# A block-wise 32x32 turn of attention's results on DVE, and w1 read in rows of 1 KB with one transfer per feature block

## The chip, the cores and the metric

The kernel runs on one core of a Trainium2 chip. What is measured is the device time of one execution in microseconds. A core has a matrix engine (PE, whose weight loads are listed apart as PEld), three engines for element-wise work (DVE, ACT, POOL), an engine that here does nothing but issue transfers (SP), and sixteen DMA engines that carry out the transfers. Each engine has its own instruction order and its list is worked through in that order; semaphores tell one engine when a result of another is there.

## The reference

Chunked attention is followed by a mixture of experts in which each token goes through all eight experts, weighted by a Sinkhorn routing.

```python
# attention: B=4, H=8, S=768, D=64; chunks of 32, context 16 left and 8 right, 8 memory tokens
for c in range(S // 32):
    q_c = q[:, :, c_start:c_end]
    k_full = concatenate([mem_k, k[:, :, l_start:r_end]])
    v_full = concatenate([mem_v, v[:, :, l_start:r_end]])
    a = softmax(q_c @ k_full.T / sqrt(D))          # per chunk
    out[:, :, c_start:c_end] = a @ v_full
x = out.transpose(0, 2, 1, 3).reshape(3072, 512)   # tokens x features
# mixture of experts: 8 experts, w_gate 512x8, w1 8x512x1024, w2 8x1024x512
P = exp(x @ w_gate - max)
for _ in range(8):
    P /= P.sum(1); P /= P.sum(0); P *= 3072 / 8
for e in range(8):
    out += P[:, e:e+1] * (maximum(x @ w1[e], 0) @ w2[e])
```

All inputs and outputs are float32 in HBM. 254.82 MB are moved in all; what counts most in arithmetic are the two products of each expert.

## The kernel before

**Attention.** The 3072 tokens are 24 blocks of 128 queries. For block n, q_n and k_n are loaded (L848, L842 to L845), kx_n, the context before and behind the block with the memory tokens (L782 to L790), and v (L921, into whatever room the planner has: v_pair, x_room, or a buffer of w2 that isn't used yet). PE turns q, k and kx (tq L1006, tk L1010, tx L806), ACT copies the turned k into kC (L1020), PE forms the scores (sp), DVE and ACT the softmax (L1083, L1089, L1108), PE turns the probabilities (ta L1126) and multiplies by v (xp L1136). DVE divides by the sums (L1154 to L1156) into xq, and the instruction at L1176 turns xq from queries x features to features x queries, in squares of 32x32, into xg, which holds 256 tokens. At the same line the features are dealt to four blocks kt: before the change, feature f of a head group went by `(f k)`, so that the four blocks take every fourth element.

**Experts.** Two xg make a unit of 512 tokens; there are six units. `build` splits x into a high and a low float16 half (ACT L513, DVE L521). The weights w1 and w2 of each expert are loaded in four parts (fp = 0 to 3) of 512 KB (`load`, L549 and L551), scaled by their largest element (`most`, L558, and `scales`), and split the same way. The first expert on the first units is done by plain products: pp (x by w1, L2037) and yp (h by w2, L2118). The others go by a scheme of seven products of 2x2 blocks (px, py, pz, then yx, yy, yz, L1590), for which `cut` adds and subtracts parts of the weights on POOL. For experts 1 to 7 all of w1 and w2 is loaded twice: once early for the largest element (w1fm, w2fm) and once for use. The routing's logits are products of xg with the gate's 512x8 weights (lp, L1391), loaded once at L2176.

**What sets the order.** Nothing waits for its turn dynamically. While the program is built, a planner takes all operations with a duration (the second argument of `add`), a priority (a due time), their dependencies and buffers, and lays out each engine's list as if those durations held. The lists that come out are fixed. Where the planner sees PE idle in the first part it puts in warm-up matmuls (`fill`, L427), whose results nobody reads. SP issues nearly all transfers, in the planned order; a transfer whose buffer isn't free holds up those behind it. So a changed duration or a changed number of instructions can move other operations to other places in the lists.

Of the kernel before, what the change touches and what calls it, by code (L numbers as in the profile page):

```python
# [233 lines left out]
def tile_chunked_attn_sinkhorn_moe(  # L234
# [27 lines left out]
    nc = tc.nc  # L262
    P = 128
    B, H, S, D = q.shape
    NM = mem_k.shape[2]
    N, DM = out.shape
    E, _, F = w1.shape
# [10 lines left out]
    KT = DM // P  # L278
# [249 lines left out]
        return b  # L528


    w1v = w1.rearrange("e (p kt) (fh fp f) -> e fp p kt fh f", p=P, fh=2, fp=FP)
    w2v = w2.rearrange("e (fh fp p) d -> e fp p fh d", fh=2, fp=FP)
    wo = {}
    known = {}

    def load(e, fp, which, prio, ahead="", eng="SP", after=()):
        shape = [P, 2, KT, P] if which == 1 else [P, 2, DM]
        place = "stage", stage
        if (e, which) == (0, 2) and ahead == "" and fp < 2:

            place = ("ws", "ss")[fp], comb
        st = buf(*place, shape, F32, f"w{which}f{ahead}_{e}_{fp}")

        queue = nc.scalar if eng == "ACT" else nc.sync

        def go():
            if which == 1:
                for fh in range(2):
                    queue.dma_start(st.t[:, fh], w1v[e, fp, :, :, fh])  # L549
            else:  # L550
                queue.dma_start(st.t, w2v[e, fp])  # L551

        return st, add(eng, 2 if which == 1 else 1, go, after, prio, [st], dma=2.1)

    def most(e, fp, which, st, deps, prio):
        def go():
# [37 lines left out]
    def cut(e, fp, which, st, ld, prio):  # L594
# [10 lines left out]
            return lambda: ws.t[:, i]  # L605

        if which == 1:
            a11, a12 = lambda: st.t[:, 0, 0:2], lambda: st.t[:, 0, 2:4]
            a21, a22 = lambda: st.t[:, 1, 0:2], lambda: st.t[:, 1, 2:4]
            ops = [  # L610
                (0, a21, a22, ALU.add),
                (1, part(0), a11, ALU.subtract),
                (2, a11, a21, ALU.subtract),
                (3, a12, part(1), ALU.subtract),
            ]
            shape = [P, 2, 7, 2, P]
        else:
            b11, b12 = lambda: st.t[:, 1, 0:DH], lambda: st.t[:, 1, DH:DM]
            b21, b22 = lambda: st.t[:, 0, 0:DH], lambda: st.t[:, 0, DH:DM]
            ops = [  # L620
                (0, b12, b11, ALU.subtract),
                (1, part(0), b22, ALU.subtract),
                (2, b22, b12, ALU.subtract),
                (3, b21, part(1), ALU.add),
            ]
            shape = [P, 2, 7, DH]
# [8 lines left out]
        if which == 1:  # L635
            parts = [
                (
                    lambda j: o.t[:, j, 0:2].rearrange("p o k f -> p (o k) f"),
                    lambda: st.t[:, 0],
                    (0.72, 0.85),  # L640
                ),
                (lambda j: o.t[:, j, 2], a22, (0.5, 0.65)),
# [45 lines left out]
    def plain1(fp, st, ld, prio):  # L688

        o = operands("w1", [P, 2, 7, 2, P], f"w1_0_{fp}")  # L690
        done = split(
            lambda j: o.t[:, j, 0:4].rearrange("p o k f -> p (o k f)"),
            lambda: st.t.rearrange("p a k f -> p (a k f)"),
            sw[:, 0, 0:1],
            [known[0, 1], ld],
            prio,
            (1.15, 1.28),
            [st, o],
        )
        wo[0, fp, 1] = (o, [done])  # L700


    def block1(e, i):
# [408 lines left out]
    def values(n, s, made):  # L1112
# [62 lines left out]
        def turn_out():  # L1175
            nc.vector.transpose(  # L1176
                gt.t[:, :, o : o + QB].rearrange("p k (c q) -> p k c q", c=CB),
                xq.t.rearrange("p c a (f k) -> p k c (a f)", k=KT),
            )

        t = add("DVE", 0.72, turn_out, [t], at + 2, [xq, gt])
        halves[g][1].append(t)
        if n % (GT // QB) == GT // QB - 1 and g > 1:

# [986 lines left out]
    for fp, s in enumerate(fetch_first(1, START)):  # L2171
# [1 line left out]
    gate_in[0] = add(  # L2173
        "SP",
        1,
        lambda: nc.sync.dma_start(  # L2176
            gate[:, :, 0:E], w_gate.rearrange("(p kt) e -> p kt e", p=P)
        ),
        (),
        30.0,  # L2180
        dma=0.3,
# [138 lines left out]
```

## Time and profile before

| | |
|---|---|
| three runs | 1918.31, 1921.56, 1921.51 us; median 1921.51 |
| the profiled execution | 1922.6 us, of which 1920.8 us are the span of the profile |
| HBM read and written over the span | 187.84 MB and 63.44 MB, 131 GB/s |
| chain that ended last, by engine | PE 93%, DVE 4%, DMA 1%, issue 1%, SP's queue 1% |
| the seven-product matmuls (px, py, pz, yx, yy, yz, L1590) | 273 ns each |
| yp (L2118) | 576 matmuls of 379 ns, 132.2 us |
| w1f, issues on SP | 72 of 256 KB |
| w1fm, issues on SP | 56 of 256 KB |

The profile is one execution, recorded instruction by instruction. The share of busy time of an engine tells what it did and not what it cost: an engine that is off the chain can be busy all the time for nothing. Three kinds of views help here: tables that split the span into stages and give each engine's busy time in each stage with PE's granted clock; lists of instructions in order of time, in which a bracket gives the idle time ahead of an instruction and what ended it; and groups of like instructions with their count, their total and their mean. In such rows "x8" is a count, "128x512 f32" the partitions, the elements per partition and the type, and SPq stands for the issuing of transfers by SP.

### The profile page before, as it was taken

The numbers are of one execution on the slowest core, as the hardware profiler recorded it, in microseconds if no ns is written. First come the engines' busy times: TensorE is split into PE (matmuls) and PEld (weight loads), VectorE is DVE, ScalarE is ACT, GpSimd is POOL, SyncE is SP. The second block draws the span as 40 slices with busy tenths as digits, with TensorE's granted clock in tenths as the row PEclk, the third lists the DMA queues.
The fourth block names the chain that finished last, engine by engine and source line by source line (L and its number), as shares of the span: only waits on it lengthen the run. The fifth ranks groups of instructions, "written<-read, shape, count | busy, mean of one in ns | idle before, by whom it ended". The sixth has DMA issues, their size and how long they took to land.

```text
span 1920.8 us, 47137 instructions
## 1 busy us (share of the span) xinstructions
PE 1899.4 (99%) x19546; PEld 1634.9 (85%) x19546; DVE 1464.2 (76%) x2420; ACT 1021.5 (53%) x1995; POOL 524.2 (27%) x549
## 2 busy tenths in 40 slices
PE   8999999999999999999999999999999999999999
PEld 7676676688888888888888888888888888888888
DVE  6886778878769866898778875898678885786565
ACT  4664554656556545645545554654554564564453
POOL 1220012543224231442124231342124232332112
PEclk9999999999999999999999999999999999999999
DMA  8677663453235332255214533245413632322321
GB/s 197 172 200 184 172 162 137 125 199 139 84 102 176 130 136 96 78 183 184 107 58 150 200 105 127 78 160 170 144 45 99 241 128 93 101 83 84 127 84 67
DMA packets 246791, 254.82 MB, mean 133 GB/s; under 512 B 113264, under 2 KB 180272, under 8 KB 242224
## 3 DMA queue, kind: packets, MB, share of 16 engines
q1 hardware_dynamic: 244452, 251.21, 41.0%
q8 instruction: 153, 2.51, 0.5%
q10 hardware_dynamic: 2124, 0.59, 0.2%
q14 instruction: 62, 0.51, 0.1%
HBM read 187.84 MB, written 63.44 MB: 131 GB/s over the span
## 4 chain that ended last, share of the span: by engine, by line
PE 93%; DVE 4%; DMA 1%; issue 1%; SPq 1%; ACT 0%; POOL 0%; DVEq 0%; POOLq 0%
PE px L1590 25%; PE yx L1590 23%; PE pz L1590 13%; PE yz L1590 11%; PE py L1590 6%; PE yy L1590 6%; PE yp L2118 4%; PE xp L1136 1%; PE pp L2037 1%; PE sp L1069 1%; DVE w L521 1%; PE warm L427 1%; DMA w1fm<-in_moe_w_dram 1%; PE ta L1126 1%; PE tq L1006 0%
## 5 line engine op out<-in xcount | busy, mean ns | idle before, releaser
L1590 PEld LDWEIGHTS <-w 128*128 128x128 f16 x7896 | 771.3, 98 | 94.6 <-issue 2.8
L1590 PEld LDWEIGHTS <-h 128*128 128x128 f16 x7056 | 690.4, 98 | 81.4 <-issue 1.5
L1590 PE MATMUL px<-x,w 128*128 128x256 f16 x4512 | 549.1, 273 | 0.3 <-DVE c L1659 0.3
L1923 POOL TENSOR_TENSOR acc<-acc,y 128x256 f32<-128x256 f32 x252 | 266.3, 1063 | 863.4 <-ACT y L1898 850.4
L1590 PE MATMUL yx<-w,h 128*128 128x256 f16 x4032 | 467.4, 273 | 1.3 <-DVE acc L1933 1.3
L1649 ACT ACTIVATE q<-px 128x256 f32<-128x256 f32 x376 | 143.0, 381 | 307.4 <-PE px L1590 302.9
L1590 PE MATMUL pz<-x,w 128*128 128x256 f16 x2256 | 277.8, 273 | 0.5 <-ACT acc L2140 0.5
L1590 PE MATMUL yz<-w,h 128*128 128x256 f16 x2016 | 233.8, 273 | 0.0
L1818 DVE TENSOR_TENSOR h<-ss,h 128x1024 f16<-128x1024 f32 x160 | 215.0, 1346 | 4.0 <-ACT h L1794 3.5
L1769 ACT ACTIVATE h<-c 128x768 f16<-128x768 f32 x168 | 140.8, 838 | 106.2 <-DVE c L1659 106.2
L1794 ACT CAST h<-ss 128x1024 f16<-128x1024 f32 x168 | 174.1, 1039 | 20.4 <-DVE ss L1758 19.6
L1758 DVE SCALAR_TENSOR_TENSOR ss<-c,ss 128x256 f32<-128x256 f32 x336 | 167.7, 499 | 8.2
L1802 DVE SCALAR_TENSOR_TENSOR h<-c,h 128x768 f16<-128x768 f32 x168 | 165.1, 983 | 9.2 <-ACT h L1769 9.1
L1659 DVE SCALAR_TENSOR_TENSOR c<-px,q 128x256 f32<-128x256 f32 x188 | 78.0, 422 | 100.2 <-PE px L1590 91.8
L1898 ACT ACTIVATE y<-yx,pscale 128x256 f32<-128x256 f32 x168 | 79.5, 473 | 114.8 <-PE yx L1590 110.8
L1590 PE MATMUL py<-x,w 128*128 128x256 f16 x1128 | 139.2, 273 | 1.3 <-DVE c L1659 1.3
L2118 PE MATMUL yp<-w,h 128*128 128x512 f16 x576 | 132.2, 379 | 0.0
L1758 DVE SCALAR_TENSOR_TENSOR ss<-c,h 128x512 f32<-128x512 f32 x168 | 121.3, 722 | 3.1 <-ACT h L1746 3.1
L1659 DVE SCALAR_TENSOR_TENSOR c<-py,q 128x256 f32<-128x256 f32 x188 | 78.3, 422 | 59.3 <-PE py L1590 53.0
L1590 PE MATMUL yy<-w,h 128*128 128x256 f16 x1008 | 116.9, 273 | 0.0
L2118 PEld LDWEIGHTS <-h 128*128 128x128 f16 x576 | 55.1, 98 | 58.7 <-issue 0.6
L513 ACT ACTIVATE w<-ws,sw 128x1024 f16<-128x1024 f32 (+1 forms) x64 | 69.2, 1088 | 62.1 <-POOL ws L602 62.1
(156 smaller groups left out, 1773.0 us busy)
## 6 DMA issues: line engine op xcount, KB each, us to landing
x<-xkeep SPq DMA_DIRECT2D x28, 1792.0 KB
akeep<-acc SPq DMA_DIRECT2D x168, 256.0 KB
acc<-akeep SPq DMA_DIRECT2D x168, 256.0 KB
w1f<-in_moe_w_dram SPq DMA_DIRECT2D x72, 256.0 KB
w2f<-in_moe_w_dram SPq DMA_DIRECT2D x32, 512.0 KB
w1fm<-in_moe_w_dram SPq DMA_DIRECT2D x56, 256.0 KB
w2fm<-in_moe_w_dram SPq DMA_DIRECT2D x28, 512.0 KB
xkeep<-x SPq DMA_DIRECT2D x6, 1792.0 KB
```

Source lines behind the costliest of these rows:

```text
L513: lambda: nc.scalar.activation(dst(0), src(), AF.Copy, scale=s),
L1590: nc.tensor.matmul(dst.t, a, b, start=(not more and n == 0), stop=(n == end), skip_group_check=more,)
L1649: lambda: nc.scalar.activation(t.t, src.t, AF.Copy, scale=DOWN),
L1659: lambda: nc.vector.scalar_tensor_tensor(c.t[:, o], src.t, DOWN, q.t, op0=ALU.mult, op1=ALU.add),
L1758: lambda: nc.vector.scalar_tensor_tensor(dst(), src(), 0.0, other(), op0=ALU.max, op1=op),
L1769: lambda: nc.scalar.activation(h.t[:, 0, 0:3], c.t, AF.Relu),
L1794: lambda: nc.scalar.copy(h.t[:, 0, 3:7], ss.t),
L1802: lambda: nc.vector.scalar_tensor_tensor(h.t[:, 1, 0:3].rearrange("p a n -> p (a n)"), c.t.rearrange("p a n -> p (a n)"), 0.0, h.t[:, 0, 0 ...
L1818: lambda: spare.tensor_tensor(h.t[:, 1, 3:7], ss.t, h.t[:, 0, 3:7], op=ALU.subtract),
L1898: (lambda: nc.scalar.activation(t.t, src.t, AF.Copy, scale=f))
L1923: lambda: nc.gpsimd.tensor_tensor(acc.t[:, cols], acc.t[:, cols], q.t, op=ALU.add),
L2118: nc.tensor.matmul(py.t, hf.t[:, hl, where[fh], o : o + P], room(fp, WIDE * wl + DM * fh, WIDE * wl + DM * (fh + 1)), start=(fp == 0 and i ...
```

## The change

1. **The turn (L1176).** The DVE transpose reads xq by `(k f)` in place of `(f k)`: each block of 32 features is a run of 32 neighbouring elements, where it was every fourth element. The instruction count stays. Its planned duration goes from 0.72 to 0.73 us.
2. **The layout of w1 and w2.** Since block kt now holds other features, the rows of w1 are dealt out to match: `w1g` gives, for one kt, the 128 features in the order of the turned x. The columns of w1 are ordered (fp fh f), so that each part fp is 256 neighbouring columns, a row of 1 KB, where it was two rows of 512 B. A load for use is four transfers of 128 KB, one for each kt, where it was two of 256 KB; a load for the largest element (`ahead`), where the order doesn't matter, is one transfer of 512 KB, where it was two. The rows of w2 are dealt to match the columns of w1. `cut` reads w1 in the new order of the buffer, [128, 4, 2, 128] for [128, 2, 4, 128], so its operands are two runs of 128 elements where they were one of 256.
3. **The first split of w1 (`plain1`).** One split of 1024 elements becomes two of 512, one for each half fh, since a half isn't contiguous in the buffer any more.
4. **The gate.** Its load becomes four transfers, one for each kt, where it was one.

```diff
--- before.py
+++ after.py
@@ -528,13 +528,14 @@
         return b
 
 
-    w1v = w1.rearrange("e (p kt) (fh fp f) -> e fp p kt fh f", p=P, fh=2, fp=FP)
-    w2v = w2.rearrange("e (fh fp p) d -> e fp p fh d", fh=2, fp=FP)
+    w1v = w1.rearrange("e (kt p) (fp fh f) -> e fp p kt (fh f)", p=P, fh=2, fp=FP)
+    w1g = w1.rearrange("e (g kt p) (fp fh f) -> e fp kt g p (fh f)", p=CH, kt=KT, fh=2, fp=FP)
+    w2v = w2.rearrange("e (fp fh p) d -> e fp p fh d", fh=2, fp=FP)
     wo = {}
     known = {}
 
     def load(e, fp, which, prio, ahead="", eng="SP", after=()):
-        shape = [P, 2, KT, P] if which == 1 else [P, 2, DM]
+        shape = [P, KT, 2, P] if which == 1 else [P, 2, DM]
         place = "stage", stage
         if (e, which) == (0, 2) and ahead == "" and fp < 2:
 
@@ -545,12 +546,16 @@
 
         def go():
             if which == 1:
-                for fh in range(2):
-                    queue.dma_start(st.t[:, fh], w1v[e, fp, :, :, fh])
+                to = st.t.rearrange("p k a f -> p k (a f)")
+                if ahead:
+                    queue.dma_start(to, w1v[e, fp])
+                else:
+                    for k in range(KT):
+                        queue.dma_start(to[:, k], w1g[e, fp, k])
             else:
                 queue.dma_start(st.t, w2v[e, fp])
 
-        return st, add(eng, 2 if which == 1 else 1, go, after, prio, [st], dma=2.1)
+        return st, add(eng, 4 if which == 1 and not ahead else 1, go, after, prio, [st], dma=2.1)
 
     def most(e, fp, which, st, deps, prio):
         def go():
@@ -605,8 +610,8 @@
             return lambda: ws.t[:, i]
 
         if which == 1:
-            a11, a12 = lambda: st.t[:, 0, 0:2], lambda: st.t[:, 0, 2:4]
-            a21, a22 = lambda: st.t[:, 1, 0:2], lambda: st.t[:, 1, 2:4]
+            a11, a12 = lambda: st.t[:, 0:2, 0], lambda: st.t[:, 2:4, 0]
+            a21, a22 = lambda: st.t[:, 0:2, 1], lambda: st.t[:, 2:4, 1]
             ops = [
                 (0, a21, a22, ALU.add),
                 (1, part(0), a11, ALU.subtract),
@@ -636,7 +641,7 @@
             parts = [
                 (
                     lambda j: o.t[:, j, 0:2].rearrange("p o k f -> p (o k) f"),
-                    lambda: st.t[:, 0],
+                    lambda: st.t[:, :, 0],
                     (0.72, 0.85),
                 ),
                 (lambda j: o.t[:, j, 2], a22, (0.5, 0.65)),
@@ -688,16 +693,19 @@
     def plain1(fp, st, ld, prio):
 
         o = operands("w1", [P, 2, 7, 2, P], f"w1_0_{fp}")
-        done = split(
-            lambda j: o.t[:, j, 0:4].rearrange("p o k f -> p (o k f)"),
-            lambda: st.t.rearrange("p a k f -> p (a k f)"),
-            sw[:, 0, 0:1],
-            [known[0, 1], ld],
-            prio,
-            (1.15, 1.28),
-            [st, o],
-        )
-        wo[0, fp, 1] = (o, [done])
+        done = [
+            split(
+                lambda j, a=a: o.t[:, j, 2 * a : 2 * a + 2].rearrange("p o k f -> p (o k) f"),
+                lambda a=a: st.t[:, :, a],
+                sw[:, 0, 0:1],
+                [known[0, 1], ld],
+                prio + 0.1 * a,
+                (0.6, 0.72),
+                [st, o],
+            )
+            for a in range(2)
+        ]
+        wo[0, fp, 1] = (o, done)
 
 
     def block1(e, i):
@@ -1175,10 +1183,10 @@
         def turn_out():
             nc.vector.transpose(
                 gt.t[:, :, o : o + QB].rearrange("p k (c q) -> p k c q", c=CB),
-                xq.t.rearrange("p c a (f k) -> p k c (a f)", k=KT),
-            )
-
-        t = add("DVE", 0.72, turn_out, [t], at + 2, [xq, gt])
+                xq.t.rearrange("p c a (k f) -> p (a k) c f", f=CH),
+            )
+
+        t = add("DVE", 0.73, turn_out, [t], at + 2, [xq, gt])
         halves[g][1].append(t)
         if n % (GT // QB) == GT // QB - 1 and g > 1:
 
@@ -2173,9 +2181,12 @@
     gate_in[0] = add(
         "SP",
         1,
-        lambda: nc.sync.dma_start(
-            gate[:, :, 0:E], w_gate.rearrange("(p kt) e -> p kt e", p=P)
-        ),
+        lambda: [
+            nc.sync.dma_start(
+                gate[:, k, 0:E], w_gate.rearrange("(g kt p) e -> kt g p e", p=CH, kt=KT)[k]
+            )
+            for k in range(KT)
+        ],
         (),
         30.0,
         dma=0.3,
```

The planner was run anew with these durations and counts, so the lists moved. PE's list differs only up to about 400 us; behind that the same matmuls stand in the same order. Its useful matmuls are the same in number, and its warm-ups are 183 where they were 194: 27 for 35 ahead of the first pp, and behind it groups of 4, 2, 6 and 5 for groups of 2, 16 and 2.

On SP, this is the first load of w1 with what stands around it (w1f_0_0 is expert 0, part 0; w2_0_2 a buffer that holds v for now; the last figures are the shape and how often the row is repeated). Before:

```order
L848 DMA q_1_188<-in_q_dram 128x8x64
L845 DMA k_1_192<-in_k_dram 128x8x64
L790 DMA kx_0_175<-in_k_dram 32x8x64 x2
L921 DMA v_pair_159<-in_v_dram 56x4x64 x4
L549 DMA w1f_0_0_286<-in_moe_w1_dram 128x4x128 x2
L549 DMA w1f_0_1_334<-in_moe_w1_dram 128x4x128 x2
L549 DMA w1f_0_2_341<-in_moe_w1_dram 128x4x128 x2
L549 DMA w1f_0_3_376<-in_moe_w1_dram 128x4x128 x2
L848 DMA q_2_432<-in_q_dram 128x8x64
```

and in the changed kernel:

```order
L856 DMA q_1_188<-in_q_dram 128x8x64
L853 DMA k_1_192<-in_k_dram 128x8x64
L798 DMA kx_0_175<-in_k_dram 32x8x64 x2
L929 DMA v_pair_159<-in_v_dram 56x4x64 x4
L554 DMA w1f_0_0_286<-in_moe_w1_dram 128x1x256 x4
L554 DMA w1f_0_1_340<-in_moe_w1_dram 128x1x256 x4
L554 DMA w1f_0_2_377<-in_moe_w1_dram 128x1x256 x4
L554 DMA w1f_0_3_425<-in_moe_w1_dram 128x1x256 x4
L856 DMA q_2_478<-in_q_dram 128x8x64
```

Eight issues of w1 have become sixteen, with the same neighbours. A little further on, w2f_0_2 and w2f_0_3 stand ahead of k_4, which stood between w2f_0_1 and w2f_0_2.

On DVE, this is the place where expert 0 begins: the splits of x_0 and of w1's four parts (L521), the reduction for x's largest element (vmax, L974, over a w2 buffer that holds v), the softmax of block 2 (sm_2, s_2), and the reductions of w2f (mxs, L558). Before:

```order
L521 SCALAR_TENSOR_TENSOR x_0_647<-xg_0_469,sx_110,x_0_647 128x512 x2
L974 TENSOR_REDUCE vmax_109<-w2_0_2_360 128x1
L521 SCALAR_TENSOR_TENSOR w1_0_0_657<-w1f_0_0_286,sw_112,w1_0_0_657 128x1024
L521 SCALAR_TENSOR_TENSOR w1_0_1_663<-w1f_0_1_334,sw_112,w1_0_1_663 128x1024
L521 SCALAR_TENSOR_TENSOR w1_0_2_666<-w1f_0_2_341,sw_112,w1_0_2_666 128x1024
L1083 TENSOR_REDUCE sm_2_769<-sp_2_719 128x2x4
L1089 TENSOR_TENSOR s_2_778<-sp_2_719,sm_2_769 128x2x4x64
L521 SCALAR_TENSOR_TENSOR w1_0_3_715<-w1f_0_3_376,sw_112,w1_0_3_715 128x1024
L558 TENSOR_REDUCE mxs_115<-w2f_0_0_651 128x1
L558 TENSOR_REDUCE mxs_115<-w2f_0_1_655 128x1
```

and in the changed kernel, where these lines are L521, L982, L1091, L1097 and L563:

```order
L521 SCALAR_TENSOR_TENSOR x_0_655<-xg_0_475,sx_110,x_0_655 128x512 x2
L521 SCALAR_TENSOR_TENSOR w1_0_0_665<-w1f_0_0_286,sw_112,w1_0_0_665 128x512 x2
L521 SCALAR_TENSOR_TENSOR w1_0_1_672<-w1f_0_1_340,sw_112,w1_0_1_672 128x512 x2
L521 SCALAR_TENSOR_TENSOR w1_0_2_676<-w1f_0_2_377,sw_112,w1_0_2_676 128x512 x2
L1091 TENSOR_REDUCE sm_2_777<-sp_2_725 128x2x4
L1097 TENSOR_TENSOR s_2_788<-sp_2_725,sm_2_777 128x2x4x64
L521 SCALAR_TENSOR_TENSOR w1_0_3_759<-w1f_0_3_425,sw_112,w1_0_3_759 128x512 x2
L563 TENSOR_REDUCE mxs_115<-w2f_0_0_659 128x1
L982 TENSOR_REDUCE vmax_109<-w2_0_2_361 128x1
L563 TENSOR_REDUCE mxs_115<-w2f_0_1_663 128x1
```

The reduction vmax has moved from ahead of w1's splits to behind them, each split has become two halves, and the softmax of block 2 stands ahead of the last part's splits as before.

On PE, this is the place at about 57 us of the profile, where the turned q and k of block 5 (tq_5, tk_5) and the product by v of block 3 (xp_3) stand between the first expert's products. Before:

```order
L1006 MATMUL tq_5_1104<-ident_98,q_5_975 128x128 x4
L1136 MATMUL xp_3_1118<-w2_0_3_386,at_3_1097 32x65 x32
L1010 MATMUL tk_5_1155<-ident_98,k_5_982 128x128 x4
L427 LDWEIGHTS ident_98
L427 MATMUL warm_1184<-ident_98 128x256
```

where fifteen more warm-ups follow, each with its weight load, and then lp_0, the logits. In the changed kernel:

```order
L1014 MATMUL tq_5_1113<-ident_98,q_5_983 128x128 x4
L1144 MATMUL xp_3_1124<-w2_0_3_389,at_3_1040 32x65 x32
L481 MATMUL sp_x_0_1161<-most_of_114,one_103 128x1
L1018 MATMUL tk_5_1165<-ident_98,k_5_986 128x128 x4
L2126 LDWEIGHTS h_0_0_826
L2126 MATMUL yp_0_1172<-w2_0_0_1096,h_0_0_826 128x512
```

Here the twelve matmuls of yp_0 and yp_1 (six each, h by w2) stand ahead of lp_0, with no warm-ups between. tx_2 (the turn of block 2's kx, at 94.76 us of the profile before) has twelve more pp and twelve more yp ahead of it, some 3.9 us of PE's work, than it had.

## The prediction

> **What bounds the kernel now.** I read the busy totals first, then the table of stages, then the start in order of time.
>
> ```profile
> PE 1899.4 (99%) x19546; PEld 1634.9 (85%) x19546; DVE 1464.2 (76%) x2420; ACT 1021.5 (53%) x1995; POOL 524.2 (27%) x549
> ...
> core 0: us, PE busy (x) PEld busy (x) DVE busy (x) ACT busy (x) POOL busy (x), PEclk, DMA share, GB/s
> 20.00:30.00 10.00, 7.80 (x125) 6.33 (x122) 9.79 (x13) 1.92 (x4) 0.00 (x0) 1.00 0.89 227
> 80.00:100.00 20.00, 17.83 (x323) 14.62 (x311) 11.23 (x19) 13.27 (x28) 5.99 (x8) 0.91 0.81 237
> 150.00:200.00 50.00, 47.57 (x861) 34.38 (x858) 35.43 (x63) 25.62 (x55) 3.51 (x5) 1.00 0.73 179
> 600.00:800.00 200.00, 200.00 (x1835) 179.21 (x1833) 154.43 (x250) 102.38 (x201) 62.80 (x65) 1.00 0.41 140
> 1600.00:1800.00 200.00, 200.00 (x1835) 179.25 (x1833) 145.63 (x238) 106.29 (x210) 49.27 (x50) 1.00 0.28 100
> ```
>
> From 600 us on PE is never idle, at full clock, with 1835 matmuls in each 200 us before and after: nothing this change does to DVE or to transfers can shorten that stretch, and PE's order is the same in both kernels there. Everything is decided in the first 400 us, where attention feeds the first units: there DVE is full at 20 to 30 us, the DMA engines are 0.73 to 0.89 busy, and PE has gaps (2.2 us in 80 to 100, 2.4 us in 150 to 200). What the change gains or loses is the position of PE's useful work when this stage ends.
>
> **Part 1, the turn.** The transpose of 512 elements takes 1112 ns, 24 times. Its price without the stride of four is not in the trace. The nearest pair of rows is one reduction that reads the same 192 elements once in order and once with a stride.
>
> ```profile
> L1176 DVE STREAM_TRANSPOSE xg<-xq 128x512 f32<-128x512 f32 x24 | 26.7, 1112 | 0.8
> ...
> L1498 DVE TENSOR_REDUCE cs<-lg 128x8 f32<-128x192 f32 x8 | 4.0, 500 | 0.3
> L1491 DVE TENSOR_REDUCE rs<-lg 128x24 f32<-128x192 f32 x8 | 2.8, 351 | 0.2
> ```
>
> The stride costs 149 ns over 192 elements, 0.78 ns each, so 0.40 us over 512: I take 0.71 us for the new turn (ends: 0.60 and the present 1.11; it reads the same elements in longer runs, so I see no reason for a loss). 24 x 0.40 is 9.5 us of DVE. Most of it lies beside a busy PE; what counts are the two turns ahead of the first expert matmul and those up to 70 us.
>
> **Part 2, the first w1 split in halves.** The start, by engines:
>
> ```profile
> 32.07 4.00 PE L427 MATMUL warm<-ident 128*128 128x256 bf16 x35
> 35.90 0.38 PE L2037 MATMUL pp<-x,w 128*128 128x256 f16 x2
> 36.48 0.61 PE L2037 MATMUL pp<-x,w 128*128 128x256 f16 x4 [0.20 <-DVE w L521]
> ...
> 41.31 0.60 PE L1126 MATMUL ta<-ident,s 128*128 128x128 f32 x4
> ...
> 19.75 1.11 DVE L1176 STREAM_TRANSPOSE xg<-xq 128x512 f32<-128x512 f32 x1
> 32.69 1.41 DVE L521 SCALAR_TENSOR_TENSOR x<-xg,sx,x 128x512 f16<-128x512 f32 x2 [0.16 <-ACT x L513]
> 34.02 1.21 DVE L974 TENSOR_REDUCE vmax<-w 128x1 f32<-128x1024 f32 x1
> 35.15 3.67 DVE L521 SCALAR_TENSOR_TENSOR w<-w1f,sw,w 128x1024 f16<-128x1024 f32 x3
> ...
> 31.93 1.33 ACT L513 ACTIVATE x<-xg,sx 128x512 f16<-128x512 f32 x2 [0.18 <-DVE sx L457]
> 33.17 3.21 ACT L513 ACTIVATE w<-w1f,sw 128x1024 f16<-128x1024 f32 x3
> ```
>
> PE fills the wait with 35 warm-up matmuls (0.114 us each) and then stands once more for DVE's split. In the change DVE reaches the splits 0.8 us sooner (two turns), the maximum of 1.21 us stands behind them, and the plan has 27 warm-ups: PE may start pp at 32.07 - 0.80 + 27 x 0.114 = 34.35. The data are there: ACT's first half at 33.1, DVE's at 34.0 (0.71 us for 512 elements, from the x rows, against 1.22 for 1024). The halves cost DVE 0.19 and ACT 0.26 us more per block, four blocks each. That is felt at once: the copy that completes kC stands behind five half splits on ACT, ending about 36.0, and PE, in order, waits there after twelve pp some 0.5 us; the softmax of block 2 then comes at 40.4 (in the order before, PE turned it at 41.31). So of 1.7 us at the first pp I keep **-1.1** (ends 0 and -1.9).
>
> **Part 3, the place at 57 to 61 us.** It carries the largest term.
>
> ```profile
> 57.35 1.91 PE L427 MATMUL warm<-ident 128*128 128x256 bf16 x16
> 60.87 1.08 PE L1391 MATMUL lp<-xg,gate 128*32 128x128 f32 x32 [1.61 <-DMA gate<-in_moe_w_gate_dram]
> 69.12 0.96 PE L1136 MATMUL xp<-x_room,at 64*32 64x65 f32 x64 [0.87 <-DVE lg L1422]
> 70.02 2.76 PE L2118 MATMUL yp<-w,h 128*128 128x512 f16 x12
> ...
> 58.61 0.56 SPq L2176 DMA_DIRECT2D gate<-in_moe_w_gate_dram  x1
> 45.04 6.85 SPq L921 DMA_DIRECT2D x_room<-in_v_dram  x8
> 24.36 4.75 SPq L921 DMA_DIRECT2D w<-in_v_dram  x8
> 14.70 7.30 SPq L549 DMA_DIRECT2D w1f<-in_moe_w_dram  x8
> 36.53 0.41 SPq L848 DMA_DIRECT2D q<-in_q_dram  x1
> ```
>
> Before, PE spends 1.91 us on warm-ups and 1.61 us waiting for the gate. In the change twelve yp matmuls (2.70 us) stand there and no warm-ups. The gate's load becomes four issues. SP gets to it sooner: its queue waits for slots that DVE frees at the start, 1.2 us sooner by the times of part 2; sixteen w1 issues of half the size carry the same bytes and take, I assume, about as long as eight (7.30 us; the q row and the slower v row bound it by 16 x 0.41 = 6.6 and 16 x 0.86 = 13.8 us). Three more gate issues at 0.5 cost 1.5. The gate lands about 0.3 later, lp starts about 61.1, and yp waits about 0.2 for w2's split: 2.70 - 0.3 - 0.2 is **-2.2** (ends -4.1 with the gate in time, and 0). The wait of 0.87 at 69 us, for results of DVE, goes, as DVE has saved four to five turns by then and its splits stand earlier: **-0.9** (ends 0 and -0.9).
>
> The plan later puts eleven warm-ups around 113 us where it had two: 9 x 0.114 is **+1.0** (0 if PE waits there anyway).
>
> **Part 4, the wait for kx.** The chain and PE show the dearest stall of this stage.
>
> ```profile
> 76.66 1.27 SPq L549 DMA_DIRECT2D w1f<-in_moe_w_dram  x2
> 90.03 1.22 SPq L549 DMA_DIRECT2D w1f<-in_moe_w_dram  x2
> ...
> 88.62 6.05 DMA kx<-in_k_dram
> ...
> 90.03 0.82 PE L2037 MATMUL pp<-x,w 128*128 128x256 f16 x6
> 94.76 0.99 PE L806 MATMUL tx<-ident,kx 128*128 128x128 f32 x4 [2.17 <-DMA kx<-in_k_dram]
> 95.54 1.49 PE L2037 MATMUL pp<-w,w 128*128 128x256 f16 x6
> ...
> 94.00:96.00 2.00, 1.24 (x7) 1.09 (x8) 0.00 (x0) 0.22 (x1) 0.00 (x0) 0.72 0.44 103
> 96.00:98.00 2.00, 2.00 (x69) 1.40 (x67) 0.48 (x1) 1.88 (x4) 0.00 (x0) 0.50 0.49 109
> 98.00:100.00 2.00, 2.00 (x23) 1.19 (x13) 1.68 (x4) 0.92 (x2) 0.00 (x0) 0.93 0.68 188
> ```
>
> The wait is 2.17 us, and the granted clock then falls to 0.72, 0.50 and 0.93 over 2 us each: 2 x (0.28 + 0.50 + 0.07) = 1.7 us more, 3.9 in all. In the change tx stands 3.9 us of work later (the rest of pp, 12 yp), but PE has gained about as much, so it arrives at the same 92 to 93 us. The last part of kx stands on SP behind four more w1 issues and three more gate issues, less the 1.2 us. I leave wait and clock as they are: **0** (ends -3.9 and +5, below). The Trainium skill, "TensorE: Matmul & The Clock Gate", section "Part 1: The HAM clock gate", has the clock halved only after an idle window of about 3.4 us. By that, a wait of this length would cost just itself, and a lost wait would bring 2.2 us instead of 3.9. The trace says otherwise here: 2.17 us were enough.
>
> **Part 5, the rest, at nothing.** The 28 later w1 loads go from 2 to 4 issues and the 28 for the maxima from 2 to 1. DVE, ACT and POOL read w1 in runs of 128 elements instead of one run, the same elements in the same instructions. All of this lies under a PE that is busy 200.00 of 200 us; if the cover went, a load late by one issue (0.5 us) would show as PE waits after 600 us, where there are none.
>
> **Sum.** -1.1 - 2.2 - 0.9 + 1.0 = -3.2. The profiled execution took 1922.6 us, 1.8 of them around its span of 1920.8; that gives 1919.4. The median of the three runs shown, 1921.51, is 1.1 lower, so I say **1918.3**.
>
> **Rivals.**
> - *The kx wait goes too.* If kx lands 2 us sooner relative to PE, both the wait and the clock dip vanish: 1918.3 - 3.9 = 1914.4. For it: larger rows on busy DMA engines (0.81), and tx stands later. Against: SP has more issues ahead of it.
> - *The lead is waited away, or the turn is no faster.* PE comes sooner to q, k and v that come no sooner, and stands 2 to 4 us longer in all; or the transpose is bound by something other than its stride and stays at 1.1. Either gives about 1921.
> - *More issues make the loads late: slower.* Seven more transfers stand ahead of the last kx. Between 76.66 and 90.03 SP issued 13 transfers in 13.4 us, 1.03 each; at that price kx lands 6 us later. The 3.9 us of work moved ahead of tx do not cover this: it decides from 3.9 / 7 = 0.56 us per extra issue on. PE then loses 2.1 us, has the longer wait with its clock dip, and meets the same lateness once more at the next q and k (gaps at 150 to 200 us): about +5, 1926.5 by the profile and 1925.5 to 1926.5 by the median. For it: v issues at 6.85 / 8 = 0.86 us; against: at 4.75 / 8 = 0.59, and the bytes are the same. The Trainium skill speaks for it: "SBUF — State Buffer", section "The DMA setup-cost knee", gives each transfer about 2 us however small it is, and asks for the largest single transfer. By its fit four of 128 KB would take 9.2 us end to end where two of 256 KB take 5.2. Here eight w1 transfers were issued in 7.30 us, so they overlap, and I count that price only in this rival.
>
> **How the numbers follow.** Forecast 0.52, spread over 1915.5 to 1921; kx gone 0.18; nothing kept 0.14; late loads 0.16. About 0.2% (3.8 us, below 1917.7 or above 1925.4) is what a measurement of this kernel can tell from no change. Faster: 0.18 and 0.22 of the forecast, 0.40. Same: 0.30 and 0.14, 0.44. Slower: 0.16. The range takes in the first rival with a margin for a gate in time (1911.5) and half of the third (1926).
>
> **What would show it.** The transpose at 0.65 to 0.75 us; first pp at 34 to 35 us; no warm-ups and yp ahead of lp near 60 us; kx still waited for near 93 us, with the clock dip behind it; equal PE counts per 200 us after 600. I am wrong if w1's sixteen issues take over 9 us, if new PE gaps of over 2 us stand between 80 and 300 us, or if PE is idle after 600 us.

## The result and the profile after

The changed kernel is slower: 1949.76 us as the median of four runs (1948.02 to 1950.31) against 1920.92 us (1918.31 to 1921.56). The ratio is 1.0151, with a 95% interval of 1.0134 to 1.0169, so 29 us are lost (26 to 32). The profiled execution has a span of 1948.5 us.

The table of stages of the changed kernel shows where (us, then busy time and instruction count of each engine, PE's granted clock, the DMA engines' mean busy share, GB/s):

```profile
24.00:36.00 12.00, 3.73 (x91) 3.07 (x74) 4.54 (x7) 0.00 (x0) 0.00 (x0) 0.88 0.28 98
36.00:42.00 6.00, 0.24 (x1) 0.24 (x2) 1.78 (x2) 0.00 (x0) 0.00 (x0) 0.50 0.61 163
42.00:48.00 6.00, 6.00 (x28) 4.33 (x28) 3.37 (x16) 3.58 (x6) 0.00 (x0) 0.50 0.80 173
...
104.00:110.00 6.00, 2.68 (x13) 2.13 (x14) 3.31 (x5) 2.92 (x7) 2.38 (x4) 0.56 0.98 344
...
600.00:800.00 200.00, 199.51 (x1829) 178.67 (x1827) 156.08 (x253) 109.06 (x215) 53.83 (x57) 1.00 0.39 134
1600.00:1800.00 200.00, 200.00 (x1835) 179.25 (x1833) 147.50 (x238) 105.31 (x206) 54.85 (x55) 1.00 0.28 96
```

Behind 600 us PE stands 0.5 us longer than before, nearly nothing, as forecast. At the start (24 to 36 us) ACT and POOL do nothing, PE and DVE are busy for about a third of the time, and the DMA engines for 0.28 of it, where they were 0.89 busy in the same stretch before. A stage in which everybody waits for transfers and the transfers use a quarter of their engines is the thing to explain. The queue of SP, which issues them, and the waits of PE and, in the last two rows, of DVE:

```profile
16.50 17.69 SPq L554 DMA_DIRECT2D w1f<-in_moe_w_dram  x16
34.31 1.17 SPq L856 DMA_DIRECT2D q<-in_q_dram  x1
...
92.38 2.35 SPq L554 DMA_DIRECT2D w1f<-in_moe_w_dram  x4
95.36 4.25 SPq L554 DMA_DIRECT2D w1f<-in_moe_w_dram  x4
99.71 1.46 SPq L856 DMA_DIRECT2D q<-in_q_dram  x1
```

```profile
41.76 1.11 PE L1014 MATMUL tq<-ident,q 128*128 128x128 f32 x4 [14.03 <-DMA q<-in_q_dram]
51.10 1.47 PE L2045 MATMUL pp<-x,w 128*128 128x256 f16 x12
107.32 1.12 PE L1014 MATMUL tq<-ident,q 128*128 128x128 f32 x4 [6.44 <-DMA q<-in_q_dram]
131.02 1.12 PE L1014 MATMUL tq<-ident,q 128*128 128x128 f32 x4 [4.24 <-DMA q<-in_q_dram]
...
432.70 1.59 PE L1598 MATMUL yx<-w,h 128*128 128x256 f16 x13 [1.59 <-POOL h L1826]
440.30 1.47 PE L1598 MATMUL yx<-w,h 128*128 128x256 f16 x12 [2.07 <-ACT y L1906]
...
35.59 1.22 DVE L563 TENSOR_REDUCE mxs<-w1f 128x1 f32<-128x1024 f32 x1 [2.38 <-DMA w1f<-in_moe_w_dram]
41.03 1.22 DVE L563 TENSOR_REDUCE mxs<-w1f 128x1 f32<-128x1024 f32 x1 [4.22 <-DMA w1f<-in_moe_w_dram]
```

The sixteen issues of w1 took 17.69 us where eight took 7.30. The q behind them went out at 34.31 (22.13 before), PE stood 14.03 us for it, and the first pp came at 51.10 (35.90 before). The same happens at 92 to 107 us and once more behind it, each time with a lower clock after the wait (0.50 and 0.56). At the start w1's own users are as late as q: DVE's reductions for w1's largest element, which the splits ahead of the first pp need, waited 12.6 us for the four parts, and the last one began at 41.03 (28.8 before), 0.73 us before PE had its q. So q in time would not by itself have brought the first pp back; that follows from the rows, no run has it.

To see where the distance arises and where it shrinks, one can count, for each moment of the profile before, the useful matmuls that have started (warm-ups left out, each weighted by its median interval) and ask how much later the other kernel reaches the same count. Worked out so from the traces, in us (the labels of the last three are those of the experiments):

| time in the profile before | 35 | 57 | 60 | 65 | 80 | 90 | 100 | 110 | 130 | 150 | 350 | 400 | 450 | 1915 |
|---|---|---|---|---|---|---|---|---|---|---|---|---|---|---|
| changed kernel | +15.0 | +15.1 | +12.2 | +12.0 | +12.2 | +20.1 | +16.9 | +22.2 | +24.0 | +23.8 | +21.8 | +21.6 | +25.8 | +27.6 |
| w1_by_rows | -0.2 | +1.0 | -1.9 | -0.5 | -0.3 | +3.9 | +1.1 | +1.5 | +3.2 | +3.0 | -3.7 | -3.9 | -1.0 | -0.7 |
| w1_one | +0.9 | +0.8 | -2.1 | -1.8 | -1.6 | -0.5 | -4.3 | -3.2 | -2.2 | -2.3 | -9.2 | -9.5 | -5.4 | -5.1 |
| lists_one | +0.5 | +0.9 | -2.0 | -2.8 | -2.3 | -2.3 | -6.0 | -5.4 | -3.5 | -3.7 | -9.6 | -9.8 | -5.7 | -5.4 |

These are single executions, and the profiled one of before was 1.7 us over its median of 1920.92, so the last column is not a verdict; the steps from column to column are what it is read for. The columns at 35, 60 and 110 lie inside stops of the kernel before (warm-ups and waits at 32.1 to 35.9, 57.3 to 60.9 and 110.3 to 111.3 us): a kernel that goes on working there looks better in them than it is, so a step is better read between columns outside, as from 57 to 65.

### The profile page after: what moved, and what is told of

Its sections match the earlier page's. It is cut to its first block, busy times and chain, and to the rows that moved or that the text cites. A ratio compares the mean times of both kernels' runs of the same rounds, so it can differ in the third digit from the quotient of the medians.

```text
span 1948.5 us, 47175 instructions
## 1 busy us (share of the span) xinstructions
PE 1906.4 (98%) x19535; PEld 1638.5 (84%) x19535; DVE 1460.0 (75%) x2424; ACT 1021.9 (52%) x1999; POOL 524.5 (27%) x549
## 4 chain that ended last, share of the span: by engine, by line
PE 90%; DMA 3%; DVE 3%; SPq 2%; issue 1%; ACT 1%; POOL 0%; ACTq 0%; DVEq 0%; POOLq 0%
PE px L1598 24%; PE yx L1598 22%; PE pz L1598 12%; PE yz L1598 11%; PE py L1598 6%; PE yy L1598 6%; PE yp L2126 5%; PE pp L2045 1%; DMA q<-in_q_dram 1%; SPq L554 1%; PE xp L1144 1%; DMA akeep<-acc 1%; PE sp L1077 1%; DVE ss L1766 1%; PE tq L1014 1%
## 5 line engine op out<-in xcount | busy, mean ns | idle before, releaser
L1826 DVE TENSOR_TENSOR h<-ss,h 128x1024 f16<-128x1024 f32 x160 | 214.5, 1343 | 3.7 <-ACT h L1802 3.6
L1766 DVE SCALAR_TENSOR_TENSOR ss<-c,ss 128x256 f32<-128x256 f32 x336 | 172.3, 513 | 8.3
```

The lines of the kernel that those rows point to most:

```text
L1766: lambda: nc.vector.scalar_tensor_tensor(dst(), src(), 0.0, other(), op0=ALU.max, op1=op),
L1826: lambda: spare.tensor_tensor(h.t[:, 1, 3:7], ss.t, h.t[:, 0, 3:7], op=ALU.subtract),
```

## The experiments

Three theories stood at the outset. **A**: a transfer whose source counts 4, 32, 256 from the outside (four groups of 32 rows of 256 elements) runs on few DMA engines. **B**: every transfer has a fixed price on SP's queue, and there are twice as many. **C**: the new lists are at fault.

**w1_by_rows**: the same four transfers of 128 KB, cut the other way.

```diff
-    w1g = w1.rearrange("e (g kt p) (fp fh f) -> e fp kt g p (fh f)", ...)
+    w1g = w1.rearrange("e (g kt p) (fp fh f) -> e fp g p kt (fh f)", ...)
...
-                    for k in range(KT):
-                        queue.dma_start(to[:, k], w1g[e, fp, k])
+                    for g in range(P // CH):
+                        queue.dma_start(to[CH * g : CH * (g + 1)], w1g[e, fp, g])
```

> The changed kernel, with each load of w1 still in four transfers of 128 KB with 1 KB rows, but cut by partition group (32 partitions with all four feature blocks each) and not by feature block; the lists of all engines stay as in the changed kernel. Theory A (few engines): a transfer whose source counts 4, 32, 256 from the outside runs on four of the sixteen DMA engines; here it counts 32, 4, 256. Then SP's sixteen issues, 17.69 us in the changed kernel, take 7 to 9 us, the first pp starts at 34 to 36 us, and the total is 1916 to 1921 us. Theory B (many issues): each transfer costs SP some 1.3 us whatever its shape; then the sixteen take 17 us again and the total stays near 1949. Theory C (the new lists): w1 comes sooner, but the total stays above 1940.

Measured: 1923.79 us, ratio 1.0015 (1.0007 to 1.0024), that is +2.9 us. The sixteen issues took 9.68 us, a little over the 7 to 9 expected, and the first pp started at 35.51. Nearly all of the 29 us is gone, with the number of transfers, the bytes and the lists unchanged: B and C fall as the main cause. Yet the total lies above the range that theory A gave, and 2.9 us stay to be explained.

**w1_groups_8, w1_groups_2 and w1_groups_16**: the changed kernel, with the source's outermost count as the only thing that varies.

```diff
-    w1g = w1.rearrange("e (g kt p) (fp fh f) -> e fp kt g p (fh f)", p=CH, kt=KT, ...)
+    w1g = w1.rearrange("e (g kt p) (fp fh f) -> e fp kt g p (fh f)", p=P // 8, kt=KT, ...)
```

> The changed kernel with each w1 transfer's source in eight groups of 16 rows in place of four of 32 (so w1's rows meet other features and the output isn't the reference's); lists, bytes, row size and number of transfers stay. Theory A: eight DMA engines, 0.66 us per transfer where four took 1.32; the sixteen issues take 9 to 12 us, the total is 1917 to 1928 us. Theory B and theory C: as the changed kernel, 17 to 18 us for the sixteen and 1947 to 1951 in all.

> The same with two groups of 64 rows (the output isn't the reference's here either). Theory A: two DMA engines, 2.6 us per transfer; the sixteen issues take 30 to 37 us, the start is later by 14 to 20 us, the next w1 loads at about 100 us are late again, and the total is 1970 to 1995 us. Theories B and C: 1947 to 1951.

> The changed kernel with each w1 transfer's source in sixteen groups of 8 rows (the output isn't the reference's); destination, bytes, rows of 1 KB, number of transfers and lists stay. Theory A: sixteen DMA engines; the sixteen issues take 9 to 10.5 us, as with the cut by partition groups (9.68), and the total is 1921 to 1927 us. Rival (the version cut by partition groups was quicker because its destination is 32 partitions of 4 KB and not 128 of 1 KB): 11 us or more, no better than with eight groups, total 1928 or more.

The stretch of the w1 loads in the table of stages, for two, eight and sixteen groups and for w1_by_rows in this order (the row for four groups, 0.28 and 98 GB/s, stands above):

```profile
24.00:52.00 28.00, 4.06 (x93) 3.26 (x91) 4.34 (x7) 0.22 (x1) 0.00 (x0) 0.62 0.14 49
18.00:25.00 7.00, 6.27 (x198) 5.11 (x193) 5.30 (x9) 2.15 (x6) 0.00 (x0) 1.00 0.50 162
18.00:26.00 8.00, 6.97 (x231) 5.75 (x232) 6.60 (x11) 2.76 (x7) 0.00 (x0) 1.00 0.59 182
16.00:24.00 8.00, 6.60 (x171) 5.21 (x169) 5.97 (x10) 4.02 (x9) 1.15 (x2) 1.00 0.85 202
```

and SP's issues of the first sixteen, in the view of the tile w1f, for two, four, eight and sixteen groups and w1_by_rows (ns, shortest/median/longest of one issue; start of the first and the last):

```profile
L554 SPq DMA_DIRECT2D w1f<-in_moe_w_dram x16: 504/2631/3045, 16.8 to 51.8; - x16
L554 SPq DMA_DIRECT2D w1f<-in_moe_w_dram x16: 522/1276/1690, 16.5 to 32.9; - x16
L554 SPq DMA_DIRECT2D w1f<-in_moe_w_dram x16: 588/589/1217, 15.0 to 25.3; - x16
L554 SPq DMA_DIRECT2D w1f<-in_moe_w_dram x16: 588/598/1675, 14.9 to 26.5; - x16
L554 SPq DMA_DIRECT2D w1f<-in_moe_w_dram x16: 312/430/1472, 15.0 to 24.4; - x16
```

| groups | DMA engines' share | GB/s | total, us | ratio to before |
|---|---|---|---|---|
| 2 | 0.14 | 49 | 2017.13 (one run) | |
| 4 (the changed kernel) | 0.28 | 98 | 1949.76 | 1.0151 (1.0134 to 1.0169) |
| 8 | 0.50 | 162 | 1928.39 | 1.0038 (1.0025 to 1.0051) |
| 16 | 0.59 | 182 | 1927.58 | 1.0045 (1.0030 to 1.0060) |

The share is close to 2/16, 4/16 and 8/16, the rate doubles and nearly doubles again, and the median issue halves from 2631 to 1276 ns, while the shortest, among the first four, took 504 and 522: with two and four groups SP stands until a transfer on few engines is through. With eight, the median of 589 ns is about that of sixteen, and the total, 1928.39, is just above the range of 1917 to 1928. This is theory A, dose by dose. The total for two groups came out 22 us above the range, because the lateness returned at each later w1 load (PE waits of 35.31, 17.23 and 8.38 us for q). With sixteen groups the expectation was missed: not 9 to 10.5 us but 12.8 from the first issue to the end of the last, and a total of 1927.58, above its 1921 to 1927 and no better than with eight. The DMA engines are not full (0.59), but now SP takes 598 ns for the median issue (three took 1.26 to 1.68 us), and 128 KB in each 0.64 us is no more than 205 GB/s; cut by partition groups an issue of the same bytes takes 430. The chain of waits has them one behind the other:

```profile
24.54 0.60 SPq L554
...
25.18 0.60 SPq L554
```

So the time of an issue depends on its shape, and the rival of that expectation holds in part: its signs came. That the even 598 ns is the price of the issue itself, and not a wait, is read from its evenness and from the rest of the run, where the median of all 144 issues is 592 ns with sixteen groups and 426 cut by partition groups. How it depends on the shape was not tried further.

The Trainium skill has this rule: "DMA: Bandwidth & Descriptors", section "Why a DMA increments its semaphore by 16 and not by 1", says that a transfer is spread over the largest number of engines up to 16 that divides the outermost count (other than 1) of both its source and its destination. Here that is 2, 4, 8 and 16 for the four kernels, and the trace agrees for the first three; the same section says nothing of the 0.59 with sixteen, which the time of SP's issues would explain.

**w1_gate_by_rows**: in addition the gate's four transfers cut the same way, by `gate[CH * k : CH * (k + 1), :, 0:E]`.

> The version with w1 cut by partition groups, and the gate's four transfers cut the same way (32 partitions outermost in place of 4 groups). Theory A again: the gate's 512 rows of 32 bytes on sixteen engines in place of four land sooner, the wait of lp (1.22 us at 62 us) falls by 0.3 to 0.8, and the total by as much or nothing: 1922 to 1924. Rival: the gate's time is that of four issues in a row (2.43 us) and nothing changes: within 0.5 us of the version without it.

Measured: 1922.14 us, ratio 1.0014 (1.0005 to 1.0023) beside 1.0015 without it. The wait of lp fell from 1.22 to 0.71 us, and the total is the same within the error; the gate's shape doesn't matter here.

**What makes the 2.9 us.** In w1_by_rows PE waits where the changed kernel waited, only less:

```profile
79.76 3.10 SPq L554 DMA_DIRECT2D w1f<-in_moe_w_dram  x4
83.44 1.91 SPq L554 DMA_DIRECT2D w1f<-in_moe_w_dram  x4
85.45 0.38 SPq L856 DMA_DIRECT2D q<-in_q_dram  x1
...
91.82 0.66 PE L1014 MATMUL tq<-ident,q 128*128 128x128 f32 x4 [3.37 <-DMA q<-in_q_dram]
```

Two theories: **I**, the number of issues ahead of q; **L**, the lists. Both have a run that holds the other still.

**w1_one** takes the lists of the changed kernel and loads w1 by one transfer: `queue.dma_start(to, w1v[e, fp])` for every load. By that view, `(kt p)`, the four rows of a partition are 128 rows apart in w1; they don't lie together, as the expectation has it.

> The lists of the changed kernel, w1 in one transfer of 512 KB per load for use (128 partitions outermost, rows of 4 x 1 KB that lie together; w1's rows then meet other features, so the output isn't the reference's). What is left of the change after the cut by partition groups, +2.9 us against before, has two theories. Theory I (issues): the w1 issues on SP hold up q and k, as at 91.8 us, where tq waits 3.37 us for a q that was issued behind eight w1 transfers. Then that wait falls below 1 us and the total is 1916 to 1920. Theory L (lists): DVE, in its new order, is what PE waits for at 406 to 414 us (0.47 and 2.07), however early PE gets there. Then these waits stay and the total is 1921 to 1924.

**before_four** takes the kernel before and only cuts its w1 transfers for use in two (the loads for the largest element stay as they were, by a branch that is left out here):

```diff
-                    queue.dma_start(st.t[:, fh], w1v[e, fp, :, :, fh])
+                    for k in (0, 2):
+                        queue.dma_start(st.t[:, fh, k : k + 2], w1v[e, fp, :, k : k + 2, fh])
```

> The kernel before with each w1 load for use in four transfers of 128 KB in place of two of 256 KB, all on sixteen engines, with the same packets of 512 bytes; lists and output as before. Theory I: at 77 to 90 us q and kx come later by four to six issues of about 0.5 us, the wait for kx of 2.17 grows to 4 or 5, and the total is 2 to 4 us above before (1922 to 1924). Theory L: within 0.7 us of before.

w1_one: 1917.52 us, ratio 0.9983 (0.9975 to 0.9992), faster than before by 3.3 us. before_four: 1922.22 us, ratio 1.0010 (1.0001 to 1.0019), slower by 1.9. Rows of w1_one, SP and PE:

```profile
14.51 3.01 SPq L551 DMA_DIRECT2D w1f<-in_moe_w_dram  x4
...
88.12 0.66 PE L1014 MATMUL tq<-ident,q 128*128 128x128 f32 x4 [1.02 <-DMA q<-in_q_dram]
409.33 1.47 PE L1598 MATMUL yx<-w,h 128*128 128x256 f16 x12 [2.06 <-ACT y L1906]
```

and of before_four:

```profile
14.44 9.87 SPq L553 DMA_DIRECT2D w1f<-in_moe_w_dram  x16
62.42 1.94 PE L1395 MATMUL lp<-xg,gate 128*32 128x128 f32 x32 [2.39 <-DMA gate<-in_moe_w_gate_dram]
```

Between four and one transfer per load lie 6.1 us (1.0015 and 0.9983 of some 1920) with the same lists, bytes and rows of 1 KB: theory I, and before_four has its sign and size with the old lists, if barely clear of no change. Where the 1.9 us arise isn't shown: the profiled execution of before_four was one of the quick ones (1919.9 us). In it the start (9.87 us for 7.30) and the gate's wait (2.39 for 1.61) grew; the wait for kx, which was expected to grow, is gone (0.32 us for v at the same place), as PE came there later. Theory L was partly right too: the wait at 409 us stayed (2.06 us), and in the table w1_one falls from -9.5 at 400 to -5.4 at 450.

**before_halves**: the kernel before with the first w1 split in halves, which brings the 183 warm-ups and most of the new order, with the loads and the turn of before.

> The kernel before with the first w1 split in halves alone; the planner then puts 183 warm-ups in place of 194, as in the changed kernel; loads and turn as before. By the prediction's terms for the lists (-1.1, -2.2 and +1.0, less the part that the turn brings) 0.5 to 2.5 us faster: 1917 to 1919.5. Theory L: the new lists themselves cost it: 1921 to 1924, with PE waits of over 2 us behind DVE at 400 to 420 us.

Measured: 1920.10 us, ratio 1.0004 (0.9996 to 1.0013): no difference, so neither total that was expected came, and no wait of over 0.3 us at 400 to 420. The gain at 57 us is there in the trace (+0.1 at 57 goes to -2.4 at 65), but PE then waits 0.89 and 0.57 us for q and k at 86 and 2.19 for q at 105 us, and by 300 us the lead is 2.3 us.

**turn_alone**: the kernel before with the new turn at the old planned duration, in the old lists.

> The kernel before with the new turn alone: planned at 0.72 us as before, so all lists are those of before; w1 is loaded in its old order, so the output isn't the reference's. By the prediction's price the turn takes 0.71 us where it took 1.11. Theory: the wait at 69 us goes (0.9) and the wait of 0.2 at the first pp; with PE's 35 warm-ups still there it gains no more at the start: 0.5 to 1.5 us faster, 1919.5 to 1920.5. Rival: sooner results on DVE change nothing, because PE's stops are set by transfers: within 0.3 us of before.

Measured: 1918.90 us, ratio 0.9996 (0.9988 to 1.0005). The turn takes 710 ns for 1112, and 9.6 us less on DVE are worth nothing that can be told from no change. The wait of 0.87 us at 69 us is gone from its trace, as expected; a wait of 1.40 us for q stands at 55 us instead.

**old_turn_one, lists_one and w1_two_queues** look for a version with few issues whose features still match the rows of w1. With the old turn the four features of a partition are neighbouring rows of w1, so one transfer per load does:

```diff
-    w1v = w1.rearrange("e (kt p) (fp fh f) -> e fp p kt (fh f)", ...)
+    w1v = w1.rearrange("e (p kt) (fp fh f) -> e fp p kt (fh f)", ...)
...
-                xq.t.rearrange("p c a (k f) -> p (a k) c f", f=CH),
+                xq.t.rearrange("p c a (f k) -> p k c (a f)", k=KT),
...
-                if ahead:
-                    queue.dma_start(to, w1v[e, fp])
-                else:
-                    for k in range(KT):
-                        queue.dma_start(to[:, k], w1g[e, fp, k])
+                queue.dma_start(to, w1v[e, fp])
```

> The changed kernel with the old turn (stride of four) and so with the old dealing of features, in which the four features of a partition are neighbouring rows of w1; each w1 load, for use or for the largest element, is then one transfer of 512 KB with 4 x 1 KB rows per partition, 128 partitions outermost, and the gate is one transfer again. w1's columns, w2's rows and the split in halves stay as changed; the planner counts one issue per load. Theory I (issues set what is lost and won): w1's first four issues take about 3 us, no wait of over 1.1 us between 80 and 100 us, total 1916.5 to 1919, faster than before, although the turn is slow. Rival (the turn carries the gain of w1_one): 24 x 0.40 us are back on DVE, total 1919.5 to 1922.

> As the last version with the old turn and one transfer per load of w1, but the planner still counts four issues per load and 0.73 us per turn, so that it lays out the lists of the changed kernel (183 warm-ups; the version before had other lists with 218). Output as the reference's. Theory: the lists and the few issues carry the gain of 3.2 us that the same lists had with the new turn, the turn itself carries 0.5 to 1.5 of it: total 1917.5 to 1919.5, faster than before. Rival (the turn carries it): 1920 to 1922.

> The version with w1 cut by partition groups, with two of each load's four transfers issued by SP and two by ACT; new turn, output as the reference's. Theory I: SP's queue is freed of half of w1's issues, the waits for q at 30 and 92 us (1.4 and 3.4) fall by half or more, total 1918 to 1922. Rival: ACT stands in order behind the waits of its own issues (for a free buffer or a free slot), delays the softmax and the copies, total 1923 to 1940.

old_turn_one: 1921.38 us, ratio 1.0007 (0.9999 to 1.0016). Its planner counts one issue per load and lays out other lists, with 218 warm-ups. Counted as in the table it leads by 6.1 us at 100 us of the profile before and is 1.9 behind at 130: PE does 37 warm-ups there and waits for x, which the planner saw coming at another time:

```profile
107.94 2.89 PE L427 MATMUL warm<-ident 128*128 128x256 bf16 x25
113.36 1.24 PE L1593 MATMUL px<-x,w 128*128 128x256 f16 x8 [2.09 <-DVE x L521]
117.85 1.47 PE L427 MATMUL warm<-ident 128*128 128x256 bf16 x12
```

lists_one, the same transfers with the numbers that give the changed kernel's lists: 1918.14 us, ratio 0.9992 (0.9983 to 1.0001). So it is 1.5 us faster at best guess, not clear of no change, and the step between it and w1_one (0.9983), in which the turn, the rows that a partition gets and the gate's load differ, lies within the error too. Theory I's claim that few issues alone make a faster kernel did not hold: it needs the lists as well. Few issues in the lists of before were not run. w1_two_queues (two of the four transfers issued by `nc.scalar`): 1930.48 us, ratio 1.0053 (1.0037 to 1.0068); PE waits 3.55 us for q at 91 and 3.97 at 116 us. Its rival's range held. In its trace ACT's pairs of w1 issues take 0.80 to 2.00 us in the first 105 us, and the q behind the two loads on SP goes out at 86.70, no sooner than in w1_by_rows (85.45), so the half queue bought nothing; whether the issues held up ACT's own work, as the rival says, isn't shown.

Of these versions only w1_one is faster than before beyond the error, and its output isn't the reference's.

## Why the prediction was wrong

**The step that failed** is the one in part 3 on the loads: "sixteen w1 issues of half the size carry the same bytes and take, I assume, about as long as eight (7.30 us; the q row and the slower v row bound it by 16 x 0.41 = 6.6 and 16 x 0.86 = 13.8 us)". They took 17.69 us, beyond both bounds. The assumption was that the same bytes need the same time. The runs showed that the bytes went through four of sixteen DMA engines (a share of 0.28, with 0.14 and 0.50 for two and eight groups), by the order in which the source is counted; the new `w1g` says so with its `g p`, four groups first, and the bounds came from q and v rows, whose transfers have 128 and 56 partitions outermost. The rival "more issues make the loads late" had the right stage and sign (a load late at 80 to 100 us, q where it named kx, and again at the next q) but the wrong price: 0.5 to 1 us per extra issue instead of a transfer that holds SP for 1.28 us each, and it had nothing at the start, where 15 of the 27.6 us arose. With w1 on all engines and as many issues, w1_by_rows is 2.9 us above before, where that rival had 5. Two of the prediction's own signs of being wrong came, the sixteen issues at over 9 us and new gaps of over 2 us behind 80 us (6.44 and 4.24); of the third, PE idle after 600 us, there are 0.5 us. Of the Trainium skill the working weighed "SBUF — State Buffer", section "The DMA setup-cost knee", and overlooked the section on the spread that is named above.

**The turn**: right. 0.71 us was taken, 0.711 measured. The price came from a reduction with another stride, so that it hits to 1 ns is luck; that the stride cost the time is borne out:

```profile
L1184 DVE STREAM_TRANSPOSE xg<-xq 128x512 f32<-128x512 f32 x24 | 17.1, 711 | 0.8
```

**The start, -1.1**: not reached in the changed kernel (+15.0). With w1 on sixteen engines it is -0.2 at 35 us in w1_by_rows and -0.8 in before_halves, but +0.9 in w1_one: of the right sign at best. These are single executions, and w1_gate_by_rows, with the same lists and w1 loads as w1_by_rows, has +3.2 there, so a term of 1.1 can't be told.

**57 to 61 us, -2.2**: about right, in the kernels with these lists. From 57 to 65 us the changed one goes from +15.1 to +12.0, so -3.1, w1_by_rows by -1.5, w1_one by -2.6 and lists_one by -3.7; before_four and turn_alone, with the lists of before, lose 2.2 and 0.5 us in the same stretch. The gate's wait fell to 0.29 us as twelve yp stand ahead of it:

```profile
72.43 2.75 PE L2126 MATMUL yp<-w,h 128*128 128x512 f16 x12
75.12 0.99 PE L1399 MATMUL lp<-xg,gate 128*32 128x128 f32 x24
76.39 0.42 PE L1399 MATMUL lp<-xg,gate 128*32 128x128 f32 x8 [0.29 <-DMA gate<-in_moe_w_gate_dram]
```

**The wait at 69 us, -0.9**: the wait went, the gain didn't come. turn_alone, in the lists of before, has no such wait, and in the new lists PE still stands for DVE there only with the old turn:

```profile
69.38 0.66 PE L1129 MATMUL ta<-ident,s 128*128 128x128 f32 x4 [1.59 <-DVE lg L1425]
...
80.75 0.63 PE L1018 MATMUL tk<-ident,k 128*128 128x128 f32 x4 [1.31 <-DMA k<-in_k_dram]
```

The first row is of lists_one, the second of the changed kernel, where a wait of 1.31 us for k came in its place; from 65 to 80 us it stays at +12. **The warm-ups at 113, +1.0**: of the right size, +1.8 from 110 to 130 us in the changed kernel and +1.0 in w1_one, though waits for x beside them (0.55 us in w1_one) are in these steps.

**The wait for kx, 0**: wrong. Where q isn't held up, the wait and its dip of the clock are gone: in w1_one the granted clock is 1.00 from 84 to 100 us, and the step from 90 (-0.5) to 100 us (-4.3) is -3.8, the 3.9 of the first rival; in the changed kernel q was late in its stead.

**The rest, at nothing**: behind 600 us right, with 0.5 us lost. Two steps between 150 and 450 us were not in the sum. PE's gaps of before at 150 to 350 us close in the new lists (w1_one: -2.3 at 150, -9.2 at 350; the gaps of 150 to 200 us alone are 2.4 of these 6.9), and at 400 to 450 us 4.1 us are lost again. That w1_one comes out at -3.3 us, where the sum said -3.2, is therefore no proof of the sum: 3.8 us of kx and 6.9 us from 150 to 350 that it had not, against 4.1 us at 400, the terms at the start and at 69 us that brought nothing, and a profiled execution of before that was long. That the number agrees is luck.

## What to carry to other kernels

Look at the outermost count of each transfer's source before its bytes or its row length: a rearrangement that puts a group of four first left three quarters of the DMA engines idle, and no total over the run showed it (the queue's packets took 41.0% of 16 engines' span before and 40.0% after), only the share in the stretch where all engines waited for it. Where one queue issues everything, a slow load is paid by what stands behind it, here q at 34, 99 and 125 us, as well as by its own users, as at the start. An engine's saved time (9.6 us of DVE in turn_alone) was worth nothing that could be measured, though a wait for that engine went with it.

## What the runs showed beside it

An issue on SP seems to have a price by shape even when nothing holds it: for 128 KB 598 ns with sixteen groups, 430 ns cut by partition groups; the 256 KB of before took 630.

A stop of PE of about 2 us was followed by a lower granted clock in some places and not in others. After 2.17 us (before, at 95 us), 2.19 (before_halves, at 106) and 2.09 (old_turn_one, at 113) the clock fell to 0.50 or 0.51 over 2 us; after 1.87 (turn_alone, at 94), 2.06 (w1_one, at 409) and 2.07 (w1_by_rows, at 414) it stayed at 1.00. So the 1.7 us that the prediction counts for the dip at kx are no fixed part of such a wait; what decides isn't shown.

DVE operations can be stretched while POOL does the subtraction h (L1826). In w1_one, at the place where the new lists lose their lead, the first of these two like DVE rows runs beside the POOL row, the second doesn't:

```profile
404.62 2.34 DVE L1766 SCALAR_TENSOR_TENSOR ss<-c,ss 128x256 f32<-128x256 f32 x1
407.28 0.55 DVE L1766 SCALAR_TENSOR_TENSOR ss<-c,ss 128x256 f32<-128x256 f32 x1
...
403.99 2.69 POOL L1826 TENSOR_TENSOR h<-ss,h 128x1024 f16<-128x1024 f32 x1 [1.44 <-ACT h L1802]
```

2.34 us for 0.55, ending 0.28 us after POOL's end. Of the 213 such rows in w1_one with nothing on POOL beside them none took more than 0.43 us; of the four beside a subtraction h two took over 2. That the lists lose their 4 us by this is read from the rows; no run took POOL's part away, so it is argued and not shown.
